# FFT phase of a gated state-space and MLP backward kernel: order of the first stage, spectra loads, and the inverse's products summed in PSUM

## The chip, the cores and the metric

The kernel runs on one core of a Trainium2 chip. The metric is the device time of one execution in microseconds (us); the time quoted for a kernel is the median of its runs. Engines: PE (TensorE matmuls; PEld its weight loads), DVE (VectorE), ACT (ScalarE), POOL (GpSimd), SP (SyncE, which here only issues DMAs). DMAs are issued on three queues, those of SP, ACT and POOL.

## What is computed

The reference computes a gated mix of two branches over a sequence of L = 2048 positions and D = 448 channels, and the gradients of its parameters for a given grad_out (written G here). Cut to what matters:

```
g = sigmoid((u * gate_w).sum(-1))                  # one gate value for each position
a = S4 branch:  K[d,l] = Re sum_n C exp(dt*A*l) dt*B   # a long convolution kernel
                y = irfft(rfft(pad(u)) * rfft(pad(K)))[:L] + u * Dskip
b = MLP branch: relu(x @ w1 + b1)**2 @ w2 + b2
out = g * a + (1 - g) * b
outputs: out and the gradients of u, A, B, C, log_dt, Dskip, w1, b1, w2, b2, gate_w
```

The gradient of the convolution kernel K is a correlation of u with g*G, and it is taken by FFT too: the spectrum of g*G times the conjugate spectrum of u, and back.

## The kernel before

All is bf16, with sums in fp32 PSUM. Positions lie on partitions as 128 x 16 (U, G, DA = g*G, DB = (1-g)*G are tiles of 128 x 16 x 448). The program is written as one list, and a scheduler turns it into one fixed order for each engine; inside an engine's queue everything runs in that order. `tc.issue_after(x)` asks the scheduler to put what it encloses behind x. Tiles with one tag (X16, Y16, R32, F17, U16, D16, K28, P14, M8) share one buffer, so a later tile waits until an earlier one is no longer read.

The parts that the change touches, in the order of the program:

- **Loads.** U, G, then the six state-space parameters by transposing DMAs (L397, into X16), then the FFT matrices (M2, MI and others), all on SP, half of U and G on ACT.
- **Gate.** DVE multiplies U with gate_w and sums (L425, 16 operations), ACT takes the sigmoid (L428), DVE makes DA (L433).
- **First FFT stage** (`fwd1`, L232): 32 matmuls with the matrix F1, two to a pair of PSUM banks; a pair is evicted to a staging buffer by ACT and DVE (`evac2`, L206, L207, L216, L218), and each of eight staged blocks is stored to HBM (gd) in two halves, one on POOL (q2) and one on SP. It runs for u (gd[0], four staging buffers in F17) and for DA (gd[1], six buffers in R32). PSUM gives three pairs in turn: two of single banks (psN) and one of a double bank (psF).
- **`transposed`** (L448, L451, L453): PE turns U and DB by 128x128 blocks, ACT and DVE copy the result into `turn`, POOL stores it to UT_d and DBT_d for the MLP later.
- **Parameters** (L492 to L514): DVE and ACT turn A, B, C and dt into Lam = exp(dt*A) and Wt.
- **`powers(gr)`** (L605 to L620): for four groups of chunks, repeated squarings of Lam between ACT (L613, L616) and DVE (L617, L618), into a record that is stored to rec_d. Two buffers take turns, one in F17 and one in R32.
- **Second FFT stage** (`spectra(q)`, q = 0..3): for w = 0 (u) and w = 1 (g*G) load a quarter of gd[w] (`load_s1`, L241; X16 for the first, Y16 for the second, alternating), 16 matmuls (`fwd2`, L251), eviction into spw (K28), and a store to sp_d. The loads of w = 0 for q = 0 and 1 are issued on POOL, the others on SP.
- **Product and first inverse stage.** `cmul` (L263 to L268) makes the complex product in two halves by six DVE operations each: two products, their sum or difference, twice. `inv1` (L282) does four matmuls for each pair of banks, summing real and imaginary part in PSUM; the result goes through a staging tile st (two buffers) to HBM (hd).
- **Second inverse stage** (L670): hd is loaded again (`load_hs`, L291, into D16 and P14) and multiplied with summing matrices; the result goes to dk_d and back as DK (K28).
- **The scan** (from L722): for each of 14 chunks DVE builds powers of the x and y sides (`build_x`, `build_y`, L722 to L736) from factors that ACT expands (`expand_x`, `expand_y`, L756 to L762), PE and ACT turn and sum them (L792, L819, L831, L861, L865, L881). The MLP's matmuls (`hidden`, L556; `project`, L964; `row_block`, L1026) fill PE between them. After it come the other gradients and the outputs.

Of the kernel before, what the change touches and what calls it, by code (L numbers as in the profile page):

```python
# [19 lines left out]
P = 128  # L20
# [143 lines left out]
class Ker:  # L164
# [36 lines left out]
    def evac2(self, dst, pr):  # L201

        if pr[2] is not None:
            self.evac(dst, pr[2][:, :, 0:D])
        else:
            self.nc.scalar.copy(dst[:, 0], pr[0][:, 0:D])  # L206
            (self.nc.scalar.copy if self.act_only else self.nc.vector.tensor_copy)(dst[:, 1], pr[1][:, 0:D])  # L207
# [5 lines left out]
    def evac(self, dst, src):  # L213
        nc = self.nc
        if self.act_only or self.evac_i % 2 == 0:
            nc.scalar.copy(dst, src)  # L216
        else:
            nc.vector.tensor_copy(dst, src)  # L218
        self.evac_i += 1


    def fwd1(self, rhs, gd, stage, act_first=0):
        nc = self.nc
        for hh in range(2):
            for q in range(4):
                self.act_only = 4 * hh + q < act_first
                st = stage[self.stage_i % len(stage)]
                self.stage_i += 1
                for j2 in range(2):
                    ps = self.pair()  # L230
                    for jj in range(2):
                        nc.tensor.matmul(ps[jj][:, 0:D], lhsT=self.F1[:, hh * 128:(hh + 1) * 128], rhs=rhs(q * 4 + j2 * 2 + jj), start=True, stop=True)  # L232
                    self.evac2(st[:, 2 * j2:2 * j2 + 2, :], ps)
                j0base = 32 * hh + q * 4
                for g2 in range(2):
                    dst = bass.AP(tensor=gd, offset=(j0base + 16 * g2) * 64 * D, ap=[[D, 64], [64 * D, 4], [1, D]])
                    (self.q2 if g2 == 0 else nc.sync).dma_start(dst, st[g2 * 64:(g2 + 1) * 64])
# [5 lines left out]
    def fwd2(self, s1, q, out):  # L243
        nc = self.nc
        M2 = self.M2[:].rearrange("p (k r m) -> p k r m", r=2, m=64)
        for ii in range(4):
            ps = self.pair()
            for ro in range(2):
                for kk2 in range(2):
                    kl = 2 * ii + kk2  # L250
                    nc.tensor.matmul(ps[ro][64 * kk2:64 * kk2 + 64, 0:D], lhsT=M2[:, 8 * q + kl, ro, :], rhs=s1[:, kl, :],  # L251
                                     start=True, stop=True, tile_position=(0, 64 * kk2))
            self.evac2(out[:, ii], ps)

    def cmul(self, out, A, B, conj_b, cm, parts=1):

        nc = self.nc
        n = 4 // parts
        cm = cm.rearrange("p (k a d) -> p k a d", k=2, d=D)
        t1, t2 = cm[:, 0], cm[:, 1]  # L260
        for h in range(parts):
            Ar, Ai, Br, Bi, Or, Oi = (x[:, n * h:n * h + n, i, :] for x in (A, B, out) for i in range(2))
            nc.vector.tensor_tensor(out=t1, in0=Ar, in1=Br, op=ALU.mult)  # L263
            nc.vector.tensor_tensor(out=t2, in0=Ai, in1=Bi, op=ALU.mult)
            nc.vector.tensor_tensor(out=Or, in0=t1, in1=t2, op=(ALU.add if conj_b else ALU.subtract))
            nc.vector.tensor_tensor(out=t1, in0=Ai, in1=Br, op=ALU.mult)
            nc.vector.tensor_tensor(out=t2, in0=Ar, in1=Bi, op=ALU.mult)
            nc.vector.tensor_tensor(out=Oi, in0=t1, in1=t2, op=(ALU.subtract if conj_b else ALU.add))  # L268

# [36 lines left out]
def kernel(ctx, tc, A_u, A_A_re, A_A_im, A_B_re, A_B_im, A_C_re, A_C_im, A_log_dt, A_Dskip,  # L306
# [75 lines left out]
    prm = [K.t("X16", [P, 8192]), K.t("Y16", [P, 8192])]  # L382
# [3 lines left out]
    def carve(n, dt=bf16, k=0):  # L386
        nonlocal o
        w = n * (2 if dt == fp32 else 1)
        if k:
            r = prm[k][:, 0:w]  # L390
        else:
            r = prm[0][:, o:o + w]
            o += w
        return r.bitcast(fp32) if dt == fp32 else r
# [7 lines left out]
    K.F1, K.M2, K.MI, K.Et = ct["F1BD"], ct["M2"], ct["MI"], ct["Etw"]  # L402
# [13 lines left out]

    s32 = const.tile([P, LT], fp32, name="s32")
# [10 lines left out]
    S.activation(g_b[:], s_b[:], ACT.Sigmoid)  # L428
# [10 lines left out]
    def transposed(src, spill):  # L439
        nonlocal nti  # L440
        for t2 in range(LT // 2):
            ps = K.ps(NT[4 + nti % 2], [P, DT, 2 * P], bf16)
            nti += 1
            for tt in range(2):
                for dt in range(DT):
                    sv = src[:, 2 * t2 + tt, dt * P:dt * P + DSZ[dt]]
                    for h in range(1 if dt < 3 else 2):
                        T_.transpose(ps[64 * h:64 * h + DSZ[dt], dt, tt * P:tt * P + P], sv, ident[:], tile_position=(0, 64 * h))  # L448
            cp = S.copy if t2 % 2 == 0 else V.tensor_copy
            lb, k = t2 // 2, t2 % 2  # L450
            cp(turn[:, lb, :, 256 * k:256 * k + 256], ps[:])  # L451
            if k == 1:
                G_.dma_start(bass.AP(tensor=spill, offset=lb * P * 2048, ap=[[2048, P], [1, 2048]]), turn[:, lb].rearrange("p a l -> p (a l)"))  # L453


    RA = K.t("R32", [P, 16384])
    Fs = K.t("F17", [P, 8704])
    stage = [[b[:, 1792 * i:1792 * i + 1792].rearrange("p (a d) -> p a d", d=D) for i in range(k)] for b, k in ((Fs, 4), (RA, 6))]
    K.fwd1(lambda j: U[:, j, 0:D], gd[0], stage[0], 5)
# [18 lines left out]
    Lr_ = carve(896, fp32)  # L478
# [9 lines left out]
    dsa = carve(4 * D, fp32, 1)  # L488
# [27 lines left out]
    K.fwd1(lambda j: DA[:, j, :], gd[1], stage[1])  # L516
# [3 lines left out]
    nc.sync.dma_start(bass.AP(tensor=DB_d, offset=0, ap=[[LT * D, P], [1, LT * D]]), flat(DB))  # L520
# [6 lines left out]
    transposed(DB, DBT_d)  # L527
    S1t = [K.t("X16", [P, 8192]), K.t("Y16", [P, 8192])]


    w1v = K.t("U16", [P, 8192])
    w1w = w1v[:, 0:7168].rearrange("p (a f) -> p a f", a=DT)
    G_.dma_start(w1w[:, 0:3], bass.AP(tensor=B_w1.tensor, offset=B_w1.offset, ap=[[F, P], [P * F, 3], [1, F]]))
    for h in range(2):
        G_.dma_start(w1w[64 * h:64 * h + 64, 3], bass.AP(tensor=B_w1.tensor, offset=B_w1.offset + 384 * F, ap=[[F, 64], [1, F]]))

# [33 lines left out]
    load_ut(0)  # L570
    load_ut(1)
# [12 lines left out]
    for rb, _, _ in psets:  # L584
        xs, ys, _, _ = fields(rb.rearrange("p (c r) -> p c r", c=4))
        for t in range(2):
            G_.memset(xs[:, :, t, :, 0], 1.0 - t)
            G_.memset(ys[:, :, t, :, 0], 1.0 - t)
# [35 lines left out]
    s1r = [S1t[i % 2][:, 3584 * (i // 2):3584 * (i // 2) + 3584].rearrange("p (a d) -> p a d", d=D) for i in range(4)]  # L624
    Pct = K.t("D16", [P, 2, 4, 2, D])
    n1 = 0

    def spectra(q):
        nonlocal n1
        for w in range(2):  # L630
            s1 = s1r[n1 % 4]
            n1 += 1
            K.load_s1(gd[w], q, s1, G_ if w == 0 and q < 2 else None)
            sp = spw[:, 2 * (q % 2) + w]
            K.fwd2(s1, q, sp)
            dst = bass.AP(tensor=sp_d[w], offset=q * 4 * 2 * D, ap=[[16 * 2 * D, P], [1, 8 * D]])
            nc.scalar.dma_start(dst, sp.rearrange("p a r d -> p (a r d)"))
    powers(0)
    spectra(0)
    powers(1)  # L640
    for q in range(4):
        if q < 3:
            spectra(q + 1)
        Pc = Pct[:, q % 2]
        K.cmul(Pc, spw[:, 2 * (q % 2) + 1], spw[:, 2 * (q % 2)], True, RA[:, 10752:10752 + 2 * 2 * D], parts=2)
        K.inv1(Pc, q, hd[0])
        if q < 2:
            powers(q + 2)
    load_const("Ew", nc.sync)
    NW2 = 32 * len(ekeys) - 4096  # L650
    Ew2 = SB[:, 10752:10752 + NW2]
    nc.sync.dma_start(Ew2, nc.inline_tensor(cs["Ew2"].astype(ml_dtypes.bfloat16), name="c_Ew2").ap())
    hsP = K.t("P14", [P, 7168])
    hss = [Pct[:, i].rearrange("p a r d -> p (a r) d").rearrange("p (g x) d -> p g x d", x=2) for i in range(2)]
    hss += [hsP[:, 3584 * i:3584 * i + 3584].rearrange("p (g x d) -> p g x d", g=4, x=2) for i in range(2)]
    for q in range(4):
        K.load_hs(hd[0], q, hss[q])
    KB = K.t("K28", [P, 14336])
# [35 lines left out]
    for k in range(2):  # L694
        G_.memset(XB[:, 4096 * k:4096 * k + 4096].bitcast(fp32), 0.0)
# [63 lines left out]
    def expand_y(c):  # L759
        S.mul(PRY.rearrange("p l w t d -> p (l w) (t d)"), ry_[c][:, 256:576].unsqueeze(2).to_broadcast([P, 5 * W2, 4]), 1.0)  # L760
        for t in range(2):
            S.mul(PIY.rearrange("p l w t d -> p (l w) t d")[:, :, t], ry_[c][:, 576:896].unsqueeze(2).to_broadcast([P, 5 * W2, 2]), 1.0 - 2.0 * t)  # L762
# [150 lines left out]
    for c in range(NCH + 1):  # L913
# [15 lines left out]
        for half in range(2):  # L929
            if c < NCH:  # L930
# [5 lines left out]
                if c + 1 < NCH:  # L936
                    if half == 0:
                        load_ry(c + 1)
                        expand_x(c + 1)
                    else:  # L940
# [443 lines left out]
```

## Time and profile before

| | |
|---|---|
| median of 5 runs | 943.79 us (938.01 to 955.57) |
| profiled execution | 952.91 us, span 951.1 us |
| busy in the span | PE 710.4, DVE 680.1, ACT 592.9, POOL 189.5 us |
| DMA | 184.5 MB, mean 194 GB/s |

The span runs from the first to the last instruction; 1.8 us lie around it. "Busy" counts the time in which an engine executes; a wait is idle time, and the profile names what ended it. The granted PE clock is given as a share of full speed. The profile covers one execution; a difference between two kernels is measured over several runs.

### The profile page before, as it was taken

To read this page: it belongs to the slowest core of one execution; us is meant where nothing else is said; L and a number is where in the kernel's file an instruction comes from. 1 tells how busy PE (TensorE), PEld (TensorE's weight loads), DVE (VectorE), ACT (ScalarE), POOL (GpSimd) and SP (SyncE) were. 2 spreads that over 40 slices of the span, in tenths; PEclk is the share of its full clock that TensorE was granted. 3 is DMA by queue.
4 is the path that set the end of the run, shared out by engine and by line. 5 is a ranking of instruction groups with operands and counts; after the bars stand their busy time and mean duration, and the time that the engine had idled before them with its cause. 6 is when DMAs were issued, how large, how long until landed. Compare 5 with 4: busy or idle time off the path is not lost.

```text
span 951.1 us, 18841 instructions
## 1 busy us (share of the span) xinstructions
PE 710.4 (75%) x7558; PEld 339.6 (36%) x7593; DVE 680.1 (72%) x1155; ACT 592.9 (62%) x944; POOL 189.5 (20%) x317
## 2 busy tenths in 40 slices
PE   3753554367888897887797877897779579878985
PEld 1311211033434443434453433542333245423443
DVE  4776978794699999899978999734159462297700
ACT  0887557526978968698668675555247535437543
POOL 1333000100102121021201303131200022433310
PEclk9965655568859998999859998999968879868998
DMA  9999783793633666546756749289999984889431
GB/s 187 277 313 364 256 315 134 283 223 116 156 75 101 148 136 138 121 98 140 153 95 152 208 117 207 84 213 275 396 290 269 291 245 143 231 252 269 139 107 44
DMA packets 162017, 184.51 MB, mean 194 GB/s; under 512 B 90884, under 2 KB 138026, under 8 KB 161018
## 3 DMA queue, kind: packets, MB, share of 16 engines
q1 hardware_dynamic: 112852, 81.21, 35.3%
q0 software_dynamic: 20432, 63.48, 20.7%
q10 hardware_dynamic: 28646, 38.62, 12.4%
q8 instruction: 59, 0.97, 0.4%
q14 instruction: 28, 0.23, 0.1%
HBM read 90.12 MB, written 72.90 MB: 171 GB/s over the span
## 4 chain that ended last, share of the span: by engine, by line
PE 33%; ACT 19%; issue 15%; DVE 14%; DMA 13%; POOL 5%; ACTq 0%; SPq 0%; POOLq 0%; DVEq 0%
PE psN L964 5%; PE psF L1101 3%; PE psX L792 3%; DMA S<-rT_d 3%; ACT R L865 3%; PE psN L556 2%; PE psN L1026 2%; PE psF L861 2%; DMA hd<-st 2%; PE psX L830 2%; ACT R L819 2%; PE psN L251 1%; DVE K L207 1%; PE psN L282 1%; ACT M L831 1%
## 5 line engine op out<-in xcount | busy, mean ns | idle before, releaser
L1101 PEld LDWEIGHTS <-S 128*128 128x128 bf16 x448 | 44.8, 105 | 62.8 <-issue 22.6
L865 ACT CAST R<-psF 128x1024 bf16<-128x1024 f32 x56 | 57.7, 1030 | 9.7 <-PE psF L861 7.7
L881 DVE TENSOR_TENSOR P<-R 128x2048 bf16<-128x2048 bf16 x42 | 49.6, 1220 | 17.7 <-ACT R L865 11.9
L964 PE MATMUL psN<-D,S 128*128 128x448 bf16 x208 | 53.0, 391 | 0.0
L1101 PE MATMUL psF<-U,S 128*128 128x448 bf16 x224 | 50.5, 375 | 2.4 <-ACT S L1096 2.4
L556 PE MATMUL psN<-S,U 128*128 128x512 bf16 x117 | 38.3, 429 | 10.9 <-ACT F L561 5.5
L861 PE MATMUL psF<-R,S 64*32 64x256 bf16 (+1 forms) x1344 | 38.1, 304 | 9.9 <-issue 4.8
L207 DVE CAST K<-psN 128x448 bf16<-128x448 f32 x36 | 22.0, 623 | 30.9 <-PE psN L251 30.0
L734 DVE TENSOR_TENSOR F<-K,F 128x2048 bf16<-128x2048 bf16 (+3 forms) x42 | 35.9, 856 | 9.7 <-ACT F L762 9.7
L1026 PE MATMUL psN<-S,U 128*128 128x512 bf16 x112 | 34.3, 411 | 8.6 <-ACT U L999 4.5
L251 PEld LDWEIGHTS <-M 128*64 128x64 bf16 x192 | 14.5, 132 | 72.6 <-issue 68.6
L722 DVE TENSOR_TENSOR X<-X,F 128x512 bf16<-128x512 bf16 (+1 forms) x70 | 37.5, 535 | 2.2 <-ACT F L756 0.3
L1095 PEld LDWEIGHTS <-S 128*128 128x128 bf16 x448 | 29.7, 102 | 25.2 <-issue 8.6
L1039 POOL DMA_DIRECT2D dhT_d<-D x28 | 20.1, 719 | 91.3 <-DVE D L1038 79.2
L733 DVE TENSOR_TENSOR K<-K,F 128x2048 bf16<-128x2048 bf16 (+3 forms) x42 | 36.4, 866 | 2.6 <-ACT F L760 1.0
L1296 DVE SCALAR_TENSOR_TENSOR F<-psN,Y 128x448 bf16<-128x448 f32 x16 | 9.9, 621 | 39.5 <-PE psN L300 39.5
L733 DVE TENSOR_TENSOR Y<-Y,F 128x2048 bf16<-128x2048 bf16 (+3 forms) x42 | 36.4, 866 | 1.9 <-DVE Y L773 0.5
L964 PE MATMUL psN<-S,D 128*128 128x448 bf16 x168 | 36.2, 367 | 1.9 <-ACT D L1031 1.9
L723 DVE TENSOR_TENSOR F<-X,F 128x512 bf16<-128x512 bf16 (+1 forms) x70 | 36.8, 526 | 1.1 <-ACT F L757 0.6
L736 DVE TENSOR_TENSOR K<-K,F 128x2048 bf16<-128x2048 bf16 (+3 forms) x42 | 36.4, 866 | 1.4
L736 DVE TENSOR_TENSOR Y<-Y,F 128x2048 bf16<-128x2048 bf16 (+3 forms) x42 | 36.4, 866 | 1.3
L734 DVE TENSOR_TENSOR F<-Y,F 128x2048 bf16<-128x2048 bf16 (+3 forms) x42 | 35.9, 855 | 0.0
(365 smaller groups left out, 1956.2 us busy)
## 6 DMA issues: line engine op xcount, KB each, us to landing
hd<-st ACTq DMA_DIRECT2D x20, 448.0 KB, 4.3
sp<-K ACTq DMA_DIRECT2D x8, 896.0 KB, 4.5
dhT_d<-D POOLq DMA_DIRECT2D x28, 256.0 KB, 4.8
R<-sp SPq DMA_DIRECT2D x8, 896.0 KB
S<-rT_d POOLq DMA_DIRECT2D x14, 512.0 KB, 5.4
R<-hd SPq DMA_DIRECT2D x16, 448.0 KB, 8.4
S<-dhT_d POOLq DMA_DIRECT2D x14, 512.0 KB, 4.0
rec_d<-F ACTq DMA_DIRECT2D x2, 1920.0 KB
```

The lines of the kernel that those rows point to most:

```text
L556: T_.matmul(ps[:], lhsT=w1w[:, dt, j * P:j * P + P], rhs=ub[:, dt], start=(dt == 0), stop=False, skip_group_check=True)
L722: V.tensor_tensor(out=hi4, in0=lo, in1=bcast_dims(pr, [0, (None, n), 1]), op=ALU.mult)
L723: V.tensor_tensor(out=Vv.rearrange("p (x a r) -> p x a r", x=2 * W2, r=2), in0=lo, in1=bcast_dims(pi, [0, (None, n), 1]), op=ALU.mult)
L733: V.tensor_tensor(out=hi, in0=lo, in1=bcast_dims(pr, [0, (None, n // 2), 1]), op=ALU.mult)
L734: V.tensor_tensor(out=Vv.rearrange("p (x a q) -> p x a q", x=rows, q=2), in0=lo, in1=bcast_dims(pi, [0, (None, n // 2), 1]), op=ALU.mult)
L736: return V.tensor_tensor(out=T4[:, :, :, n:2 * n], in0=T4[:, :, :, n:2 * n], in1=V4, op=ALU.add)
L861: T_.matmul(psz[32 * ii:32 * ii + m, t, 256 * s:256 * s + 256], lhsT=DKc[64 * t:64 * t + 64, s, g, 2 * ii:2 * ii + 1 + par].rearrange("p i ...
L865: S.copy(zb[:, :, :, gg].rearrange("p s t n -> p t s n"), psz[:].rearrange("p t (s n) -> p t s n", s=2))
L881: lastp = V.tensor_tensor(out=pr.rearrange("p s t g n -> p s t (g n)"), in0=zv, in1=(xb if r == 0 else rev_dim(xb, 2)), op=ALU.mult)
L964: lastm = T_.matmul(ps[:, 0:D], lhsT=hblk[j][:, P * tt:P * tt + P], rhs=ws[:, j, :], start=(w == 1 and j == 0), stop=(j == FT - 1))
L1026: T_.matmul(ps[:], lhsT=w2Tw[:, jp, dt, j % 2], rhs=dblk[:, dt], start=(dt == 0), stop=False, skip_group_check=True)
L1101: lastm = T_.matmul(ps[:, 0:width], lhsT=hh[:, t, :], rhs=(DB2[:, t, :] if w == 0 else U[:, t, 0:D + 1]), start=(t == 0), stop=(t == LT - 1))
```

## The change

- `fwd1` of u moves ahead of the gate in the program, and the sigmoid is put behind the last eviction of u's first stage that ACT does alone (the first five blocks).
- The parameters' scratch moves from X16/Y16 to R32, so that Y16 is free early. All loads of `load_s1` go on SP: those of u for q = 0, 1 right after the first stage of DA, later ones as the second stage frees its buffer. u's loads use Y16, those of g*G X16.
- The turn of DB, its spill DBT_d and the store DB_d move from ahead of the spectra to between the products of q = 0 and the next (behind the first spectrum of g*G); the loads of w1 and UT_d move behind the products, to just ahead of the scan.
- `cmul` and `inv1` are replaced for this convolution by `cprod` and `inv1p`: DVE makes the four products alone, and their sums and differences are made by eight matmuls for each pair of banks (a negated copy of the imaginary matrix, MIn, gives the sign). The product buffers lie in U16 and R32.
- The memsets of the power records are put behind the first stage of DA.
- `expand_y(1)` is split: the factors of the first four levels are expanded in the first half of chunk 0.

```diff
+    K.F1 = ct["F1BD"]
+    RA = K.t("R32", [P, 16384])
+    Fs = K.t("F17", [P, 8704])
...
+    K.fwd1(lambda j: U[:, j, 0:D], gd[0], stage[0], 5)
+    u_ev = K.last_ev
     s32 = const.tile([P, LT], fp32, name="s32")
...
-    S.activation(g_b[:], s_b[:], ACT.Sigmoid)
+    with tc.issue_after(u_ev.ins):
+        S.activation(g_b[:], s_b[:], ACT.Sigmoid)
...
-    Lr_ = carve(896, fp32)
+    Lr_ = RA[:, 14336:16128].bitcast(fp32)
...
-    dsa = carve(4 * D, fp32, 1)
+    dsa = RA[:, 10752:14336].bitcast(fp32)
...
-    K.fwd1(lambda j: DA[:, j, :], gd[1], stage[1])
+    lf1 = K.fwd1(lambda j: DA[:, j, :], gd[1], stage[1])
+    SX, SY = prm, K.t("Y16", [P, 8192])
+    s1r = [b[:, 3584 * i:3584 * i + 3584].rearrange("p (a d) -> p a d", d=D) for b in (SY, SX) for i in range(2)]
+    def s1_load(w, q):
+        return K.load_s1(gd[w], q, s1r[2 * w + q % 2])
+    for q in range(2):
+        s1_load(0, q)
     transposed(U, UT_d)
...
-    nc.sync.dma_start(bass.AP(tensor=DB_d, offset=0, ap=[[LT * D, P], [1, LT * D]]), flat(DB))
...
-    transposed(DB, DBT_d)
...
-    G_.dma_start(w1w[:, 0:3], bass.AP(tensor=B_w1.tensor, offset=B_w1.offset, ap=[[F, P], [P * F, 3], [1, F]]))
...
-    load_ut(0)
-    load_ut(1)
...
+            with tc.issue_after(lf1.ins):
+                G_.memset(xs[:, :, t, :, 0], 1.0 - t)
+                G_.memset(ys[:, :, t, :, 0], 1.0 - t)
...
+    def cprod(self, out, A, B, h):
+        nc = self.nc
+        for i, (x, y) in enumerate(((0, 0), (1, 1), (1, 0), (0, 1))):
+            nc.vector.tensor_tensor(out=out[:, i], in0=A[:, 2 * h:2 * h + 2, x, :], in1=B[:, 2 * h:2 * h + 2, y, :], op=ALU.mult)
+    def inv1p(self, pr, q, hd):
...
+        mats = (MI[:, 0], MI[:, 0], MI[:, 1], self.MIn)
...
+            for i in range(4):
+                for kk2 in range(2):
+                    r0 = 64 * kk2
+                    nc.tensor.matmul(ps[kk2][:, 0:D], lhsT=mats[i][r0:r0 + 64], rhs=pr[r0:r0 + 64, i, ii, :],
+                                     start=(i == 0), stop=(i == 3), tile_position=(r0, 0))
...
+    spectrum(0, 0)
+    s1_load(1, 0)
+    s1_load(1, 1)
     powers(0)
-    spectra(0)
+    spectrum(0, 1)
+    spectrum(1, 0)
+    f10 = K.last_f2
     powers(1)
     for q in range(4):
         if q < 3:
-            spectra(q + 1)
-        Pc = Pct[:, q % 2]
-        K.cmul(Pc, spw[:, 2 * (q % 2) + 1], spw[:, 2 * (q % 2)], True, RA[:, 10752:10752 + 2 * 2 * D], parts=2)
-        K.inv1(Pc, q, hd[0])
+            if q > 0:
+                spectrum(0, q + 1)
+            ls1 = spectrum(1, q + 1) or ls1
+        for h in range(2):
+            pr = prd[(2 * q + h) % 3]
+            K.cprod(pr, spw[:, 2 * (q % 2) + 1], spw[:, 2 * (q % 2)], h)
+            K.inv1p(pr, 2 * q + h, hd[0])
+        if q == 0:
+            nc.sync.dma_start(bass.AP(tensor=DB_d, offset=0, ap=[[LT * D, P], [1, LT * D]]), flat(DB))
+            with tc.issue_after(f10.ins):
+                transposed(DB, DBT_d)
         if q < 2:
             powers(q + 2)
...
+    w1v = K.t("U16", [P, 8192])
...
+        mx = G_.memset(XB[:, 4096 * k:4096 * k + 4096].bitcast(fp32), 0.0)
+    with tc.issue_after(mx.ins):
+        load_ut(0)
+        load_ut(1)
...
                     if half == 0:
                         load_ry(c + 1)
                         expand_x(c + 1)
+                        if c == 0:
+                            expand_y(1, 0, 4)
+                    elif c == 0:
+                        expand_y(1, 4, 5)
                     else:
                         expand_y(c + 1)
```

## The prediction

> **What bounds the kernel now.** I read the slices of the page first, then busy time by stretch, then the chain that ended last, then each engine in order of time.
>
> ```profile
> span 951.1 us, 18841 instructions
> ...
> DVE  4776978794699999899978999734159462297700
> ...
> PEclk9965655568859998999859998999968879868998
> DMA  9999783793633666546756749289999984889431
> ```
>
> A slice is 23.8 us. All the edits but one lie in the first eight slices (the FFT phase). There the DMA engines are full for four slices (to 95 us), DVE is not; from slice 8 on DVE is at 9. So the FFT phase is a lead-in to a stretch bound elsewhere, and what it gets shorter by moves everything behind it, unless the hand-over stalls.
>
> ```profile
> 67.10:94.00 26.90, 9.64 (x72) 5.23 (x72) 16.32 (x35) 22.54 (x32) 10.15 (x19) 0.50 1.00 353
> 94.00:104.30 10.30, 8.55 (x48) 4.41 (x48) 8.46 (x17) 7.95 (x15) 0.00 (x0) 0.72 0.65 222
> 104.30:186.50 82.20, 40.83 (x144) 11.71 (x143) 68.28 (x139) 48.50 (x94) 6.07 (x3) 0.51 0.66 252
> ```
>
> Columns: length, then busy time of PE, PEld, DVE, ACT, POOL, the granted PE clock, DMA share, GB/s. From 67 to 94 us DVE works 16.3 of 26.9 us with the DMA engines full; from 104 to 186 it works 68.3 of 82.2 us (83%).
>
> ```profile
> 80.97 0.56 POOL L540 DMA_DIRECT2D S<-UT_d  x1
> ...
> 85.97 1.07 POOL L241 DMA_DIRECT2D X<-gd  x2
> ...
> 93.98 0.96 PE L251 MATMUL psF<-X,M 128*64 128x448 bf16 x4 [15.33 <-DMA X<-gd]
> ```
>
> The second FFT stage begins at 93.98 because its first load is issued on POOL at 85.97, behind four DBT_d stores, w1, UT_d and eight memsets, and then takes 8 us. The gd[0] it reads was stored from 47 us on.
>
> ```profile
> 26.20 0.21 ACT L428 ACTIVATE g_b<-s_b 128x16 bf16<-128x16 bf16 x1 [13.94 <-DVE s_b L427]
> ...
> 231.68 0.38 DVE L734 TENSOR_TENSOR F<-K,F 128x256 bf16<-128x256 bf16 x1 [9.66 <-ACT F L762]
> ```
>
> ```profile
> 180.03 4.89 DMA hd<-st
> 185.00 0.97 ACT st L206 x2
> ```
>
> The first fence is from the engines in order of time, the second from the chain. At the front ACT idles 13.9 us for the gate while u's evictions wait behind it; at the end the last eviction into st waits for a store, and L722 of the scan starts at 186.5; later DVE waits 9.7 us for the y factors.
>
> **Front: u's first stage ahead of the gate.** ACT takes u's evictions from about 12.3 (after its table load). It gets only three PSUM pairs: in the built order PE then turns u (four groups at DVE's pace, to 23.4 in the trace) before it goes on. The next five pairs take 4 x 0.85 + 0.8 = 4.2 us, to 28 (before: 32.6). Then ACT has exp of log_dt (28.7, was 35.1) and four L451 copies 2.06 us apart (PE 0.95, ACT 0.91, two hand-overs), to 36. Set 4 needs the first of four stage buffers back: its SP store cannot issue before 31.39, where SP comes free of parameter transposes and constants, and lands 4.7 later, at 36.1. So set 4 to the first pair of set 5 end at 38.2, and the sigmoid, now behind them, with a table load of 1.28 in front, gives g at about 40 instead of 26.4: a wait of 14 us is given to the gate. Behind it on ACT stand the rest of u's evictions, on DVE L433 (16 of g G, 4.0 us), then the first stage of g G. That began at 44.5 before with g G ready at 30.7, so 13.8 us of slack covers it; I get 45.5. Without that cover the 14 us go into gd[1] and into every load of w=1.
>
> DVE fills its idle time with the parameter work, but this needs the transposed Ci: issued at 25.73, X loads land in 7.8 to 10.1, so 34.7 against 36.4 before, a gain of 1.7; with L433 and five of u's evictions now in front of the second half, the parameters are ready at 52.5 (was 51.1). Fourteen evictions (11 x 0.535, 3 x 1.0) and six parameter operations (4.6) follow, 13.5 us, with 1 to 2 us of waits on stage buffers (3.5 before): the powers start at 67.5 (was 67.1). The front gains nothing; bounds: 3 us earlier (all idle time after 26 filled bar the raw loads) to 6 later.
>
> A rule that speaks against this order: the Trainium skill, ScalarE: Activation LUTs (What ACT_TABLE_LOAD costs), asks to batch functions by table set and gives a switch as a 1283 ns load plus a 1380 ns drain. The trace shows the load (1.28 us at 33.27) and the next activation 0.01 us behind it. The built order has four loads for three; by the page one more is an estimated 2.7 us ahead of the gate, and the sum would be 1.4 us less.
>
> **Loads on SP, and what leaves the front.** u's loads for q=0,1 go on SP after its stage-1 stores (44.5 + 4.7 to 8.8 landing, so issue by 54, data by 61 at 6.9). The stores of g G queued behind that wait are not due before 53.6, so it hides. w1 (1.6 MB), UT_d (1 MB) and DBT_d (2 MB) leave the time to 94: 4.6 MB, at 353 GB/s 13 us of full DMA engines. The memsets leave the load's way. PE does u's spectra from 65.5. The first spectrum of g G needs gd[1] landed: Y loads of it issued at 73.3 before; now DB_d and a load of u stand ahead, 3.6 MB at 353 GB/s = 10 us from 68.5 to 74, land at about 82 (bounds 80, a load alone at 6.9; 92, with 18.4, the longest gd load of the page).
>
> DVE meanwhile: by the built order 17.6 us of work from 67.5 to the first product, by the start-to-start times of the rows: 10 evictions at 0.535 (5.4), 2 of two banks at 1.0, 15 power steps (L617, L618) at 0.335 (5.0), four L606/7 at 0.6 (2.4), four L608/9 at 0.54 (2.2), an L451 (0.6). Up to the spectrum of g G it is 14.2 plus some 2 of waits for ACT squares, so 83.7: DVE and load arrive together. The spectrum's matmuls and evictions follow, first product at 88 against 104.3: **16.3 gained** (bounds 19.2 and 6).
>
> **Products, PSUM sums, and DBT.** DVE: 32 products instead of 48 operations of the same 128x896 form, 16 x 0.535 = 8.6 us less. Moved in: four L451 copies at 0.61 = 2.4. By the order, 60.4 us of DVE work remain from the first product to the last st eviction, against 68.3: products 17.1, 22 evictions 11.8, 6 of two banks 6.0, L451 2.4, 45 power steps 15.1 and 20 short ones at 0.21, L606 to L609 3.5, the scan's seeds 0.3. At the old 83% that is 72.8 us. Against it: PE. Inverse matmuls double, 64 more at 0.90/4 to 0.93/4 per form, half clock: 64 x 0.19 = 12 us; the DBT turns move in, 8 x 1.43 = 11.4. PE then is busy 40.8 + 23.4 = 64 of some 76 us, near DVE's 60: not yet the bound, but each inverse pair of banks comes 0.75 us later and waits in PE's order behind turns and spectra. And DMA: 252 GB/s x 82.2 = 20.7 MB, less 2 of early loads, plus DBT_d and UT_d 3.1, in 76 us: 287 GB/s, below the 353 to 406 that full stretches show, so landings (hd<-st 4.3 median) lengthen but do not bound. I take 4 us for both: 76.8, **5.4 gained**, so the scan starts at 164.8 (was 186.5). Bounds: 9.4 gained (nothing for PE and DMA), or all 23.4 us of PE on the chain, 68.3 - 8.6 + 13.9 + 23.4 = 97, 14.8 lost.
>
> A rule on the queues: the Trainium skill, DMA: Bandwidth & Descriptors (Issuing engines are not separate DMA queues), says that queues of SP, ACT and POOL share the same 16 engines and that another issuer saves issue time alone. The rows agree in part: the X load took 8 us at a DMA share of 1.0, but 15 us before it were POOL's program order. By the rule the queue change is an estimated 1 us; leaving w1, DBT and UT out of the way is the rest.
>
> **Hand-over to the scan.** w1 now issues when the last inverse matmul frees its buffer, together with the last hd stores and the eight hd loads (D, P; DMA share 0.97). 1.6 MB at 211 to 294 GB/s is 5.4 to 7.6 us; PE's use of D has 3.2 us of cover (it waits that long for Y at 206.4), P 6. I take **3.5 lost** (0 to 8). The scan's first loads of UT hide behind 34 us.
>
> **y factors.** DVE's 9.66 wait falls, but its next operation, L881 at 249.94, waits 6.83 for ACT's L865, which follows dk_d; the stall moves there and becomes 16. I take 0; 2.5 at most, from four ACT operations fewer ahead of L865.
>
> **Sum.** 16.3 + 5.4 - 3.5 = 18.2 us off the profiled execution's 952.91 (span 951.1, 1.8 around it): 934.7. That execution is 1% above the median 943.79, runs lie between 938.0 and 955.6. On the median: 943.8 - 18.2 = 925.6, say **926**. About 1% (9.4 us) is what a measurement here tells from no change.
>
> **Rivals.** (1) *The DMA engines stay the bound.* For: share 1.00 to 94, and 1.01 at 406 GB/s from 120.0 to 132.4; the DBT and UT traffic only moves, and st has two buffers. Against: 0.66 over the stretch. Price: the X load lands at 92 (6 gained, not 16.3), second part 5.4, hand-over 8 lost: 3.4, so 940. (2) *PE becomes the bound, slower.* PE runs in order with a granted clock of 0.51 from 104 to 186; inverse and turns alternate with spectra, each waiting for banks that DVE or ACT must empty, so that its 23.4 us add to the chain: 16.3 - 14.8 - 3.5 = 2 lost; with the X load at 92, 12 lost: 956. It decides once more than 12 of the 23.4 us are uncovered with the load late (6 + 9.4 - 3.5). Against: PE idled 41 of 82 us there, and 64 of 76 still leaves 12. (3) *Hand-over worse than the gain in the lead-in*, 8 lost: within the main case, 930.
>
> **How the numbers follow.** Main case 0.75 (its own range 917 to 933: first term down to 11 or up to 19.2, second 9.4 at best), DMA 0.14, PE 0.11. The range reaches from 916 to 942, which takes in the DMA case and half of the spread of runs. Faster by over 1%: the main case and a little of DMA, 0.76; within 1%: most of DMA and some of PE, 0.14; slower 0.10.
>
> **What would show it.** In the profile after: sigmoid near 40; the first spectrum matmul near 65, of w=1 near 82; first product (the 128x896 multiplies) near 88; the scan's first L722 near 165; ACT's y factors no longer waited for, and a longer wait of DVE for R. Wrong if the first product comes after 95, if the products' stretch is over 85 us, or if PE idles under 6 us in it.

## The result and the profile after

The changed kernel is slower: 953.7 us (median of 35 runs, 945.8 to 961.2) against 946.25 (64 runs, 936.4 to 955.6); the ratio is 1.0086, with a 95% interval of 1.0066 to 1.0105. I had forecast 926. The ratios leave out runs more than 1.5% above the fastest of their kernel (six of the 35 here), and the profiles of e8, e10 and e15 are of such runs. Since the profile shown of the kernel before is of an execution well above its median, I laid the changed kernel beside a second profile of the kernel before (span 939.4 us, called "before" from here on; run b0 below).

The page of the changed kernel, its span and slices:

```profile
span 951.7 us, 18950 instructions
...
DVE  4597867593689999999877999855229754278800
...
PEclk9777555658769899899867997799869789979999
DMA  9989664995527756445942966359998996789531
```

A slice is 23.8 us. Against the page of the kernel before, the DMA engines are freer in slices 5 and 6, from 95 us on (6, 6 after 7, 8), and fuller in 7 and 8 (4, 9 after 3, 7). DVE is less busy there: 8, 6, 7, 5 in slices 5 to 8, where it had 9, 7, 8, 7, and its row of nines begins in slice 13 instead of 12. On DVE the FFT phase has become emptier, not shorter.

The front, from the engines in order of time:

```profile
38.94 1.01 ACT L478 COPY S<-psX 128x1024 bf16<-128x1024 bf16 x1 [5.06 <-DMA UT_d<-S]
42.16 0.91 ACT L216 CAST F<-psF 128x896 bf16<-128x896 f32 x1 [2.21 <-DMA gd<-F]
...
42.85 0.62 DVE L207 CAST F<-psN 128x448 bf16<-128x448 f32 x1 [5.35 <-DMA gd<-F]
...
45.69 0.21 ACT L455 ACTIVATE g_b<-s_b 128x16 bf16<-128x16 bf16 x1
...
80.02 0.33 SPq L243 DMA_DIRECT2D Y<-gd  x1
80.77 0.80 SPq L243 DMA_DIRECT2D X<-gd  x2
...
89.37 0.96 PE L253 MATMUL psN<-X,M 128*64 128x448 bf16 x4 [7.26 <-DMA X<-gd]
...
98.38 0.62 DVE L276 TENSOR_TENSOR U<-K 128x896 bf16<-128x896 bf16 x1
```

The gate came at 45.7 us (I had said 40). It stands on ACT behind u's evictions, and ACT waited twice ahead of them: 5.06 us for a store of the turned u, which held its copy back to 38.94, and then to 42.16 for the store that gives a stage buffer back. DVE's eviction waited 5.35 us for such a store too. The powers started at 71.5, not 67.5. The loads of g G's first stage were issued at 80.8, right behind a reload of u's first buffer (Y) that could not issue before PE had read it, and w=1's first spectrum matmul ran at 89.4 (82 forecast). First product at 98.4 (88).

The end of the FFT phase: DVE in order of time, POOL's loads of UT_d and w1, then the chain of waits.

```profile
184.00 0.62 DVE L207 CAST st<-psN 128x448 bf16<-128x448 f32 x1 [5.89 <-DMA hd<-st]
...
187.94 1.16 DVE L207 CAST st<-psN 128x448 bf16<-128x448 f32 x2 [2.32 <-DMA hd<-st]
189.10 0.43 DVE L757 TENSOR_TENSOR X<-X,F 128x512 bf16<-128x512 bf16 x1
...
174.04 1.06 POOL L559 DMA_DIRECT2D S<-UT_d  x2
...
186.68 0.78 POOL L687 DMA_DIRECT2D U<-in_B_w_dram  x1 [4.21 <-PE psN L289]
```

```profile
179.34 8.15 DMA hd<-st
187.54 0.40 issue
187.94 1.17 DVE st L207 x2
189.18 9.22 DMA hd<-st
198.55 0.56 SPq L316
...
200.46 9.41 DMA D<-hd
```

Two hd stores of 448 KB took 8.2 and 9.2 us, the first beside two UT_d loads issued at 174.0, the second beside w1. The loads of hd (D) could issue only at 198.6, behind the last store. The scan started at 189.1 and not at 165.

The stages by start times, as differences of rows (us). "Quarter" is the first product of each of the four rounds; the last eviction is that into st; Ew is the first matmul of the second inverse stage; P<-R is DVE's first multiply of R. e4, e9 and e14 are versions of the changed kernel told of below.

| stage | before | changed | e4 | e9 | e14 | changed less before |
|---|---|---|---|---|---|---|
| to the first product | 103.5 | 98.4 | 97.2 | 93.3 | 88.1 | -5.1 |
| quarter 1 to 2 | 15.4 | 14.8 | 14.8 | 17.5 | 18.1 | -0.6 |
| quarter 2 to 3 | 26.1 | 33.3 | 32.8 | 32.5 | 32.9 | +7.2 |
| quarter 3 to 4 | 24.8 | 23.0 | 23.5 | 23.6 | 26.7 | -1.8 |
| quarter 4 to last eviction | 15.0 | 18.4 | 15.3 | 15.2 | 15.4 | +3.4 |
| last eviction to Ew | 12.0 | 17.8 | 12.0 | 12.0 | 12.0 | +5.8 |
| Ew to P<-R | 52.3 | 49.5 | 53.6 | 53.2 | 53.5 | -2.8 |
| P<-R at | 249.1 | 255.2 | 249.2 | 247.3 | 246.7 | +6.1 |

So 5.1 us were won ahead of the products, 7.2 lost between the second and third quarter, and 9.2 at the hand-over, of which 2.8 were cover. 6.1 of some 8 us are there by P<-R. In kernels whose instructions are in one order up to the first product (the changed one, e2, e4, e7) it came at 97.2 to 100.9, so a difference under 4 us between two single profiles says little.

### The profile page after: what moved, and what is told of

It reads as the page before. It is cut to its first block, busy times and chain, and to the rows that moved or that the text cites. A ratio compares the mean times of both kernels' runs of the same rounds, so it can differ in the third digit from the quotient of the medians.

```text
span 951.7 us, 18950 instructions
## 1 busy us (share of the span) xinstructions
PE 729.5 (77%) x7626; PEld 344.6 (36%) x7657; DVE 669.0 (70%) x1139; ACT 594.2 (62%) x949; POOL 187.2 (20%) x315
## 4 chain that ended last, share of the span: by engine, by line
issue 35%; PE 17%; DMA 12%; DVE 10%; ACT 9%; POOL 8%; SPq 0%; POOLq 0%; ACTq 0%; DVEq 0%
PE psF L1141 3%; DMA hd<-st 3%; DMA S<-rT_d 2%; PE psN L1004 2%; POOL dhT_d L1079 2%; DMA X<-gd 1%; DVE U L276 1%; POOL br_d L1006 1%; PE psN L253 1%; POOL rT_d L586 1%; DMA S<-dhT_d 1%; DMA D<-hd 1%; PE psN L307 1%; ACT R L901 1%; DMA U<-in_A_A_im_dram 1%
## 5 line engine op out<-in xcount | busy, mean ns | idle before, releaser
L917 DVE TENSOR_TENSOR P<-R 128x2048 bf16<-128x2048 bf16 x42 | 49.5, 1220 | 16.1 <-ACT R L901 10.2
L768 DVE TENSOR_TENSOR K<-K,F 128x2048 bf16<-128x2048 bf16 (+3 forms) x42 | 36.4, 866 | 13.5 <-DMA K<-dk_d 10.8
L1135 PEld LDWEIGHTS <-S 128*128 128x128 bf16 x448 | 29.7, 102 | 24.0 <-issue 9.0
L867 ACT COPY M<-psX 128x1024 bf16<-128x1024 bf16 x26 | 26.6, 1022 | 17.1 <-PE psX L866 17.1
L854 PE MATMUL psX<-ident,X 128*128 128x128 bf16 x224 | 19.6, 237 | 20.2 <-DVE X L761 13.0
```

The source lines that it names most:

```text
L768: V.tensor_tensor(out=hi, in0=lo, in1=bcast_dims(pr, [0, (None, n // 2), 1]), op=ALU.mult)
L917: lastp = V.tensor_tensor(out=pr.rearrange("p s t g n -> p s t (g n)"), in0=zv, in1=(xb if r == 0 else rev_dim(xb, 2)), op=ALU.mult)
```

## The experiments

**b0. The kernel before, once more.** No edit.

> The kernel before, once more, for a profile that can be laid beside that of the changed kernel stage by stage (the one shown at first took 952.9 us, 0.7% above the median of 946.25). Theory A, the loss of the changed kernel lies between the first product and the first multiply of dk: here first product within 2 us of 104.3, the scan's first multiply within 3 us of 186.5, first P<-R multiply near 249, span near 943. Theory B, the loss lies behind that (the y factors, the scan): here those marks would be as late as in the changed kernel (scan 189, P<-R 255) and the gain would come after 255 us.

First product 103.5, scan 186.3, P<-R 249.1, span 939.4. Theory A: most of the loss stands by P<-R.

**e1. The loads of g G first.**

```diff
...
-    spectrum(0, 0)          # reloads u's first buffer
-    s1_load(1, 0)
-    s1_load(1, 1)
+    s1_load(1, 0)
+    s1_load(1, 1)
+    spectrum(0, 0)
+    s1_load(0, 2)
```

> The changed kernel with the two loads of g G's first stage (X<-gd) put on the sync queue ahead of the reload of u's first buffer. Theory A (a wait at the head of the queue): that reload waits for PE to have read its buffer (80.0 us) and holds back the X loads, which would otherwise issue near 72.5; w=1's first spectrum matmul moves from 89.4 to about 82, the first product from 98.4 to about 91, and the time falls by 4 to 7 us (0.5 to 0.7%). Theory B (PE, with twice the inverse matmuls and the turns, sets the stretch's end): first product earlier, scan start within 2 us of 189, time within 0.3%. Theory C (DMA engines): the X load issued earlier lands no earlier than 87, time the same.

```profile
77.85 1.60 SPq L243 DMA_DIRECT2D X<-gd  x2
...
86.24 0.76 PE L253 MATMUL psN<-X,M 128*64 128x448 bf16 x6 [2.10 <-DMA X<-gd]
```

Issued 2.9 us sooner, not 8 (the last stores into gd[1], which it reads, are issued until 72.3 us). First product 94.3 (98.4), scan 189.0, time 952.07, ratio to before 1.0066 (1.0026 to 1.0106). The wait at the queue's head is real and small; what it gave did not reach the scan, as theory B has it.

**e2. w1 behind the hd loads: first try.** w1's loads on the sync queue in place of GpSimd's.

> The changed kernel with w1's three loads on the sync queue behind the eight loads of hd, not on GpSimd's queue as soon as the products' buffer is free (186.7 us). Theory A (hand-over): the last hd<-st store took 9.2 us beside w1 and the D loads were issued at 198.6; here it lands in about 3.5 and they are issued near 193; the first Ew matmul moves from 205.7 to about 200, dk and the scan's first P<-R (255.2) come 5 us sooner, time 4 to 6 us less (0.5%). Theory B (dk has slack): those marks move, the time does not (within 0.3%). If w1 then comes too late, the first matmuls with U (229.1) move behind 231 and the time rises.

In the built order two of the three stood ahead of the hd loads again (issued from 189.4, hd's from 199.5). 959.73 us, ratio 1.017 (1.0114 to 1.0227). It tests nothing; it was done again as e4.

**e3. The gate early.**

```diff
-    with tc.issue_after(u_ev.ins):
-        S.activation(g_b[:], s_b[:], ACT.Sigmoid)
+    S.activation(g_b[:], s_b[:], ACT.Sigmoid)
```

> The changed kernel with the sigmoid free to go as soon as the gate's sums are there, instead of behind u's first-stage evictions. Theory A: g comes near 27 instead of 45.9, g G's multiply ends near 32, gd[1] is stored 5 to 10 us sooner, the parameters are ready 3 to 5 us sooner (powers at 67 to 68 instead of 71.5); but w=1's load stays behind the reload that waits for PE, so the first product moves by 3 to 5 us only, and the time by 2 to 5 us (0.2 to 0.5%). Theory B (DMA engines full to 90 us anyway, 0.95 and 0.83 of their time): the marks before 70 move, the first product stays within 2 us of 98.4 and the time within 0.2%.

The sigmoid came at 29.7, the powers at 70.0 (71.5). But the scheduler now put DB_d's store and the reload ahead of the X loads, which issued at 87.1; first product 98.7, scan 193.8, 957.05 us, ratio 1.0118 (1.0045 to 1.0191). Neither theory had this; the edit was repeated with those queues fixed (e14).

**e4. The tail cleared.**

```diff
-    G_.dma_start(w1w[:, 0:3], ...)        # and two more
+    with tc.issue_after(lhs.ins):         # lhs: the last load of hd
+        nc.sync.dma_start(w1w[:, 0:3], ...)
...
-        load_ut(0)
-        load_ut(1)
+    with tc.issue_after(lw1.ins):
+        load_ut(0, nc.sync)
+        load_ut(1, nc.sync)
```

> The changed kernel with w1 and the two UT_d loads (2.6 MB) put on the sync queue behind the eight hd loads, by an order that the scheduler keeps (in e2 it had put w1 ahead of them again, so e2 told nothing). Theory A (loads moved into the hand-over): the stores hd<-st land in 4 us instead of 8 to 9, the last eviction into st at about 182 to 184 instead of 187.9, the D loads at about 188 instead of 198.6, the first Ew matmul near 196 (205.7), P<-R near 249 (255.2): 5 to 7 us less, a time near 947. Theory B (two st buffers and rec_d's stores hold the tail by themselves): last eviction within 1.5 us of 187.9, D loads near 194, 3 us less at most. Theory C (work behind 210 us takes it back, as w1 is needed at 229): the marks to 200 move, P<-R does not.

Its chain of waits, then SyncE and PE in order of time:

```profile
178.17 5.02 DMA hd<-st
```

```profile
187.93 2.52 SPq L316 DMA_DIRECT2D D<-hd  x4
...
195.58 1.34 PE L706 MATMUL psN<-D,M 128*32 128x448 bf16 x12
```

The same store takes 5.0 instead of 8.2 us, the last one (issued at 184.88) no longer holds the D loads back beyond 187.93, so that they issue 10.6 us sooner, Ew comes at 195.6, P<-R at 249.2. 946.7 us, ratio 1.0033 (1.0001 to 1.0065). Theory A, to within a microsecond at each mark: moving w1 and UT_d cost 5 to 6 us, over half of the loss. The run moves both at once and does not price them apart.

**e5. The turns ahead again.**

```diff
+    nc.sync.dma_start(...DB_d...)     # ahead of the powers
+    transposed(DB, DBT_d)
...
-            nc.sync.dma_start(...DB_d...)
-            with tc.issue_after(f10.ins):
-                transposed(DB, DBT_d)
```

> The changed kernel with (1-g)G turned and stored ahead of the powers, as before, not between the products. Theory A (PE's order lengthens the stretch): from first product to the last eviction into st 89.5 us fall by 8 to 11 (8 turn groups of 1.43 us and their hand-overs), but the first product comes 3 to 6 us later; scan start near 184, time 2 to 5 us less. Theory B (the stretch is held by DMA waits at its end, by st's stores at 176 to 188): the scan starts within 2 us of 189, time the same within 0.4%.

Slower still: 956.89 us, ratio 1.0167 (1.0091 to 1.0243). Quarter 2 to 3 shrank to 28.2 us (33.3), but quarter 1 to 2 grew to 21.9 (14.8), with the powers' first group ending at 119.8 (108.9), and quarter 3 to 4 to 26.5 (23.0); the scan started at 195.3. Neither theory had this: ahead of the powers the turns cost at least as much. Since the powers move too, the run is no price of the turns alone.

**e6. The products alone, on the kernel before.** `cprod` and `inv1p` put in for `cmul` and `inv1`, nothing else.

> The kernel before with one part of the change alone: four products of each kind into a buffer and the sums in PSUM by twice the inverse matmuls. DVE then has 32 products for 48 operations, 8.6 us less; PE 64 matmuls more. Theory A (this part gains by itself, what I forecast at 5.4): first product at 103.5 as in the kernel before, scan start near 181 to 183 (186.3), time 3 to 5 us less (0.4%). Theory B (PE pays it back): stretch of 80.5 us or more, scan start 186 to 190, time 0 to 4 us more.

```profile
104.30:187.40 83.10, 53.86 (x208) 18.08 (x208) 59.74 (x123) 48.91 (x94) 6.08 (x3) 0.54 0.66 250
```

(Columns as in the stretches above: length, busy PE, PEld, DVE, ACT, POOL, PE clock, DMA share, GB/s.) DVE works 59.7 us instead of 68.3, as reckoned, and the stretch is not shorter: quarters at 104.3, 119.6, 145.1 and 171.9 against 103.5, 118.9, 145.0 and 169.8. 949.57 us, ratio 1.0058 (1.0017 to 1.01). Theory B: nothing gained. Some 5 us are even lost; P<-R is only 0.8 us later (249.9), so most of that lies behind it and stays unexplained. The edit takes work off DVE and puts work on PE at once; no run did the first alone.

**e7. The y factors whole.** The five levels of chunk 1 together again in the changed kernel.

> The changed kernel with the split of the y factors (chunk 1's four levels early, the fifth later) undone. Theory A (it changes nothing): scan start and P<-R within 2 us of 189.1 and 255.2, time within 0.4% of the changed kernel (953.7). Theory B (the split puts its ACT work ahead of R's casts, and the changed kernel's further 6 us between 396 and 510 us come from it): P<-R near 252, time 4 to 6 us less.

957.38 us, ratio 1.0147 (1.0095 to 1.02), P<-R at 261.2. The gate alone was 2.9 us later in this profile, which the edit cannot do. It excludes theory B. The marks of A (within 2 us) are missed as well, by 3.5 at the scan (192.6) and 6 at P<-R; its size is left to e11.

**e8. Tail cleared, sums on VectorE.** e4 with `cmul` and `inv1`.

> e4 (tail cleared) with the products summed on VectorE and half the inverse matmuls again, as before; the turns, the early loads and the gate's place stay changed. The chain that ended last holds 22.8 us of PE and 37.3 of DVE in the changed kernel's products' stretch against 7.6 and 43.1 in the kernel before. Theory A (PE in lock-step with DVE and ACT ate the gain): PE on the chain falls to about 14, the scan starts at 180 to 183 (184.8), time 3 us under e4 (about 943). Theory B (DVE's work sets the stretch): 8.6 us more of it, scan start 188 to 192, time 3 to 6 us over e4.

945.06 us, ratio 0.9977 (0.9942 to 1.0013), scan at 188.3, quarter 2 to 3 still 32.8 us. By the time no difference from e4 can be told (1.0033, the intervals overlap). The scan start, of a single profile, is not weighed. Taking 64 matmuls off PE, with the 8.6 us given back to DVE, did not bring the 7 us between quarters 2 and 3 back.

**e9. Tail cleared, g G's loads first.** e4 with the edit of e1.

> e4 with e1's order of the loads as well (X<-gd ahead of the reload of u's buffer). In e1 the first product came 4.1 us sooner and the scan started no sooner, behind stores that waited for w1 and UT_d. Theory A (that tail hid it): scan start 181 to 183 (184.8), first Ew matmul about 193, time 2 to 4 us under e4 (946.7). Theory B (the chain of the powers, which starts when the parameters are ready at 72 and is not touched, sets the stretch's end): scan start within 1.5 us of 184.8, time within 0.3% of e4.

944.44 us, ratio 0.9998 (0.9968 to 1.0029): all of the loss is made good. First product 10.2 us ahead of the kernel before, scan 2.6 (183.7). Against e4 that is theory B: the scan starts 1.1 us sooner, and the intervals of the two ratios overlap.

**e10. Each inverse matmul twice, in the kernel before.**

```diff
-                for ri in range(2):
+                for n, ri in enumerate((0, 0, 1, 1) if two else (0, 1)):
```

> The kernel before with every inverse matmul of the first convolution issued twice into the same sum (hd then holds twice the product; its work and bytes are unchanged): 64 matmuls more on PE, nothing less on DVE. Theory A (PE's 12 us lie on the chain in part): scan start 5 to 8 us later than 186.3, time 4 to 8 us more. Together with e6 (the same matmuls and 8.6 us less of DVE: scan start 187.4) that prices the two halves of the edit. Theory B (PE idles 41 of 82 us and hides it): scan start within 2 us of 186.3, and then e6's lost gain is not PE's.

```profile
104.40:185.90 81.50, 55.73 (x208) 17.90 (x207) 68.16 (x139) 48.36 (x94) 6.08 (x3) 0.54 0.67 253
```

(`two` is set for the first convolution alone.) PE works 55.7 us instead of 40.4, and the stretch takes 81.5 us instead of 82.8. 949.04 us, ratio 1.001 (0.9969 to 1.0052). Theory B: PE's idle time hides the doubled matmuls.

**e11. The y factors' split alone, in the kernel before.**

> The kernel before with the split of the y factors alone. My forecast was 0 (2.5 at most gained): DVE's wait for L762 (9.66 us) goes, and its wait for ACT's R grows by as much. Time within 0.3% of the kernel before, first P<-R multiply within 2.5 us of 249.1. Rival: the split moves ACT's order in the scan and costs 0.4% or more.

950.44 us, ratio 1.0011 (0.9966 to 1.0056): no difference that can be told, as forecast; 0.45% either way stays possible. P<-R came at 246.3, 2.8 us sooner than before and so just outside the mark; e10, which has no split, shows 245.6.

**e12. The fourth group's squarings left out of e9.**

> e9 with the squarings of the last group of powers left out (its copies and its store stay; rec_d's last two chunks then hold wrong powers). Theory A (the powers' chain paces the stretch): the last store of rec_d and the last eviction into st come 8 us or more sooner (182.1 to 174 or less). Theory B (spectra and products with their evictions set the end): the last eviction into st moves by less than 3 us.

Its store of rec_d went out at 168.7 (176.3 in e9), the last eviction came at 188.0 (182.1). Neither theory had 6 us later. The scan's first multiplies moved ahead of the last evictions in this build (176.3), so the end is not a clean test; nothing here speaks for theory A.

**e13. rec_d's last store on another queue.**

```diff
-        nc.scalar.dma_start(bass.AP(tensor=rec_d, ...
+        (nc.sync if gr == 3 else nc.scalar).dma_start(bass.AP(tensor=rec_d, ...
```

> e9 with rec_d's last store (960 KB, issued on ScalarE's queue 0.4 us ahead of an hd store at 176.3) on the sync queue. Theory A (the hd store waits behind it in that queue): the hd store lands in 3 us instead of 5, DVE's and ACT's waits for it (2.0 and 3.0, 0.8 and 3.6 us) fall to under 3 together, last eviction at about 179.5 (182.1), scan start 181. Theory B (bytes in the DMA engines, whatever the queue): marks within 1 us.

```profile
176.89 0.62 DVE L207 CAST st<-psN 128x448 bf16<-128x448 f32 x1 [2.03 <-DMA hd<-st]
181.99 1.16 DVE L207 CAST st<-psN 128x448 bf16<-128x448 f32 x2 [3.48 <-DMA hd<-st]
```

The waits stay (2.0 and 3.5 us; 2.0 and 3.0 in e9), the scan starts at 183.5 (183.7). 944.67 us, ratio 0.9963 (0.9921 to 1.0006). Theory B: the queue is not it. That agrees with the Trainium skill, DMA: Bandwidth & Descriptors (Issuing engines are not separate DMA queues), by which queues share the same engines.

**e14. Gate early, tail cleared, g G's loads first.** The edits of e3, e4 and e1, with DB_d's store held behind the X loads.

> e9 with the gate early again (as e3) and DB_d's store behind g G's loads. Theory A (the powers' chain, from the parameters on): parameters ready at 67 to 69 instead of 72.2, scan start 180 to 181 (183.7), time 2 to 3 us under e9 (944.4), that is 0.3% under the kernel before. Theory B: g G's first stage is stored sooner, first product near 90, but the scan's start stays within 1.5 us of 183.7 and the time within 0.3% of e9.

```profile
74.33 0.81 SPq L243 DMA_DIRECT2D X<-gd  x2
...
88.12 2.75 DVE L276 TENSOR_TENSOR U<-K 128x896 bf16<-128x896 bf16 x5
...
135.65 0.44 DVE L625 TENSOR_TENSOR R<-R 128x128 bf16<-128x128 f32 x1 [7.00 <-DMA rec_d<-R]
...
177.16 0.62 DVE L207 CAST st<-psN 128x448 bf16<-128x448 f32 x1 [3.88 <-DMA hd<-st]
```

This version beats both kernels: 942.25 us, ratio to before 0.9937 (0.99 to 0.9973). Its first product is where I had forecast that of the changed kernel (88.1), and its scan starts at 182.7, 3.6 us ahead of the kernel before, where the first product is 15.4 ahead. Against e9 the scan (1 us sooner) fits theory B and the time (0.9937 after 0.9998) theory A.

**e15. The same with rec_d's last store on the sync queue.**

> e14 with e13's edit: everything undone that held the gain back and could be undone, u's first stage ahead of the gate's work, early loads, products and turns kept. Theory A (both): scan start near 178, time 4 to 6 us under the kernel before (0.5%). Theory B (neither): 944, no difference that can be measured.

942.82 us, ratio 0.9934 (0.9899 to 0.9969): e14's time again, and nothing from the queue. The scan started at 178.9, but ahead of the last eviction, which stayed at 181.0.

**e16. The third group's squarings left out of e14.**

> e14 with the squarings of the third group of powers left out (rec_d's chunks 8 to 11 then hold wrong powers; copies and stores stay). Theory A (the third group's chain, in program order with the evictions of the later spectra on VectorE and ScalarE, paces them): the last quarter's products start 6 us or more sooner than in e14 (165.8) and the last eviction into st comes at 174 or sooner (181.2). Theory B (the stores at the tail and the DMA engines set it, as in e12): the last eviction within 2 us of 181.2.

The last quarter began at 162.8 (165.8) and the last eviction came at 181.7 (181.2). Not the 6 us of theory A; and the scan's first multiplies moved ahead of the last evictions in this build (170.2), so the end is not a clean test. Undecided.

**e17. The fourth group later on VectorE.**

```diff
+        with (tc.issue_after(K.p2.ins) if gr == 3 else nullcontext()):
             V.tensor_tensor(out=ua, ...     # and the next three
```

> e14 with the fourth group's first multiplies behind the third group's sixth squaring on VectorE (nothing left out). In e14 VectorE waits 7.0 us at 135.65 for rec_d's store of the second group, whose buffer the fourth takes, with the third group and the products of the second quarter behind it. Theory A: that wait goes, the third group's store comes at 154 to 156 (159.5), the scan starts near 179 (182.7), the time falls by another 2 to 4 us (about 939, 0.8 to 0.9% under the kernel before). Theory B (the fourth group becomes late instead, and its store is what the tail waits for): scan start within 1.5 us of 182.7, time within 0.3% of e14.

```profile
135.78 0.42 DVE L637 TENSOR_TENSOR R<-P 128x256 f32<-128x256 f32 x1 [5.78 <-ACT P L635]
```

The wait of 7.0 us for the store is gone; DVE waits 5.8 us for ACT at the same place, where ACT stands behind two copies of the turns (130.6 and 133.1). Scan 182.8, 941.45 us, ratio 0.9962 (0.9927 to 0.9997). By these marks theory B.

## Why the prediction was wrong

The step that failed is the overlap in the products' stretch: I let the lead of the first product run through it and took DVE's saved work off its length. It took 90.7 us where I had 76.8. Beside it, two waits were missing from the lead-in and the hand-over was mis-sized. Two of my three signs of being wrong came: a first product after 95 and a stretch over 85 us.

*The y factors (0 forecast).* Right as far as can be told: e11 shows none beyond its 0.45%. Only the place was wrong. DVE now waits 10.80 us for dk and 2.90 for R, where I had put 16 on R:

```profile
241.64 0.43 DVE L768 TENSOR_TENSOR K<-K,F 128x512 bf16<-128x512 bf16 x1 [10.80 <-DMA K<-dk_d]
...
255.21 2.36 DVE L917 TENSOR_TENSOR P<-R 128x2048 bf16<-128x2048 bf16 x2 [2.90 <-ACT R L901]
```

*First product at 88, 16.3 gained.* It was 98.4: 5.1 us gained, under the lower bound of 6. Two terms failed. The gate came 5.7 us later than I had it: I had the stage buffer's store landing at 36.1, and ACT waited for one until 42.16, behind a wait of 5.06 us for the turned u that I had not counted at all. The "13.8 us of slack" was used up: powers at 71.5. And I counted the reload of u ahead of the X loads as bytes, not as an instruction that waits for PE with the X loads behind it. With the loads in order and the gate free again (e14), the powers start at 67.4, as I had them (67.5), and the first product comes at 88.1. That fits the sum of the lead-in from the powers on. That it meets 88 to 0.1 us is luck, and e14 gives up the gate's new place, so it does not show that the front could have held. The table load ahead of the gate, for which the Trainium skill, ScalarE: Activation LUTs (What ACT_TABLE_LOAD costs), adds a drain of 1380 ns, cost its 1.28 us alone here too: it starts at 44.40 and the sigmoid at 45.69.

*Products' stretch 76.8 us, 5.4 gained.* It took 90.7, 7.9 more than before, 3.4 of that at its end, where e4 takes it back. This is the largest miss: I let the first product's gain run through to the scan one for one and then shortened the stretch by DVE's work. The experiments show neither. DVE's 8.6 us less, with PE's 64 matmuls more, shortened nothing (e6), the matmuls by themselves cost nothing (e10), and a first product 10.2 or 15.4 us earlier gives 2.6 or 3.6 at the scan (e9, e14). Most of the lead goes between the second and third quarter: 6.4 of the 7.6 us that e9 loses, 6.8 of the 11.8 of e14, which loses 2.7 and 1.9 in the rounds on either side. It takes 30.7 us (e17) to 35.0 (e16) in every version of the changed kernel but e5 and e3 (39.5), and 24.3 to 26.1 in the four that keep the turns ahead of the powers and the loads as before (before, e6, e10, e11). What the first have there and the others not is the later half of the turns, with its copies on ACT and DVE between the spectra's evictions; with the turns ahead it is 28.2 us (e5). The products' form is not it (e8: 32.8), nor the gate's place (e14: 32.9), nor the loads at the tail (e4: 32.8). That is as far as the runs carry the cause: no run moved the turns alone in the kernel before, and in e5 the powers moved too. Busy time from the second to the third quarter, of the changed kernel and of the kernel before (columns as above):

```profile
113.20:146.50 33.30, 22.43 (x100) 8.15 (x97) 21.59 (x46) 19.66 (x31) 2.17 (x4) 0.50 0.65 246
...
118.90:145.00 26.10, 12.80 (x50) 3.83 (x47) 19.26 (x40) 14.77 (x25) 0.00 (x0) 0.50 0.73 286
```

Of the 7.2 us more, DVE works 2.3 and idles 4.9. I had priced PE and DMA at 4 us together over the whole stretch, as work, while PE, ACT and DVE each run in their order and wait for one another. The chain of waits points the same way: summed over its pieces, PE holds 22.8 us of the changed kernel's stretch, against 7.6 before, though PE is busy for only 59.8 of the 90.7 us.

So my second rival ("PE becomes the bound") had the right place and, in part, the wrong cause: PE idles 31 of the 90.7 us and DVE 27, so no single engine was the bound. That its 956 lies near the 953.7 is in part luck, since over half of the loss is the hand-over's. What remains open is which order of PE, ACT and DVE there would let the lead through; one change of it (e17) moved nothing, and e12 and e16 are no clean tests.

*Hand-over 3.5 lost (0 to 8).* It was 9.2: 5.8 from the last eviction to Ew and 3.4 ahead of the last eviction; 2.8 of that were cover behind Ew. My 3.5 had the cover in it, so the term was 6.4, a mis-sized one. The mechanism was as I wrote it, w1 beside the last stores; I had missed that the UT_d loads, which I said "hide behind 34 us", slow the stores on which the evictions wait: the store of 8.2 us landed at 187.5, within a microsecond of w1's issue at 186.7, and so had UT_d beside it and hardly w1. e4 shows both together.

*The sum.* By stages: 5.1 gained in the lead-in, 4.8 lost over the quarters (7.2 less 0.6 and 1.8), 9.2 lost at the hand-over, 2.8 of cover behind it, together 6.1 us lost at P<-R. The medians differ by 7.5 us; the rest lies behind 255 us, where no single profile settles it.

## What to carry to other kernels

Before you add a gain at the head of a stretch to the end's time, mark the stretch's inner rounds and ask at each which in-order engine it waits for: of 15.4 us of lead the scan here kept 3.6 (e14). A load that leaves a crowded time is not gone; look at what is issued just before the hand-over, since 448 KB stores there took 8 to 9 us beside 2.6 MB of loads that were first read 40 us later, and the first of them 5 without. When a queue's instruction waits for a buffer, what stands behind it on that queue waits too (the loads of g G issued 2.9 us sooner without the reload ahead of them, e1), so put the loads that wait for no buffer first.

## What the hardware showed unexpectedly

Taking 8.6 us off an engine that is busy 82% of a stretch (with 13.5 us more on PE), or adding 15.3 us of PE's busy time at a granted clock of 0.53 to 0.54, left that stretch's length at 81.5 to 83.1 us (82.8 before). And one order of instructions can take quite different times: behind the FFT phase the kernel before and e6 have the same order on DVE and ACT, and from P<-R to PE's last matmul took 683.5 and 694.4 us in two profiles of the first and 696.0 in e6. That is more than the whole effect in question, so the end of a single profile prices nothing here; medians do, and marks in its first 255 us to within some 4 us.
